# Instruction orders from tables in place of a list scheduler, in a two-layer attention and mixer kernel

## The chip, the cores and the metric

The kernel runs on one core of a Trainium2 chip. The metric is the device time of one execution in microseconds; the time before is the median of three runs. A core has five engines that run their own instruction streams and meet at semaphores: TensorE (PE), VectorE (DVE), ScalarE (ACT), GpSimd (POOL) and SyncE (SP), which here only issues DMAs.

## The reference

Two layers over x of 2048 rows and 448 columns (bfloat16). Each layer is an attention block with 16 heads of 28 columns, then a mixer with an MLP; both read a normed x and add to x.

```
x = x + _A_ref(_layernorm(x), wqkv, wo)
x = x + _B_ref(_layernorm(x), w1, w2, w3, w4)      # the pair of lines twice, with the same weights

_A_ref: q, k, v = split(x @ wqkv);  softmax(q k^T / sqrt(28)) v, heads joined, @ wo
_B_ref: h = gelu(layernorm(x) @ w1)                # 448 -> 448
        hs = (four column groups of h shifted by -1, +1, -2, +2 rows) @ w2
        x1 = x + hs
        return x1 + gelu(layernorm(x1) @ w3) @ w4  # 448 -> 1792 -> 448
```

All of x, the weights and the keys and values stay in the core's memory; x is cut into 16 tiles of 128 rows.

## The kernel before

**The work.** Keys, queries and values are projected tile by tile (`kq_proj`, `v_proj`). Scores are computed transposed: 128 keys by 512 queries (256 in the last units of layer 1) for one head with a 32-row strip of the array (L1243), four heads side by side. ACT takes the exponential of two or three banks of scores at once (L1269, 821 instructions) and writes PT. For 50 tiles DVE computes the exponential instead, with five instructions of its own (`t_dexp`, L1159 to L1172). PT then multiplies the values (L1318, in one of four 32-column strips) into bank 5; `t_norm` divides and transposes, `t_outproj` multiplies with wo and adds to x. The mixer follows in `t_mixA` (w1, tanh form of gelu with L1433 on ACT between DVE's steps), `t_x1` (w2, second norm with a power on POOL, L1568) and `t_mixB` (w3, gelu, w4). The gelus of several tiles are collected into nine long ACT instructions (L1650), since a change between the exponential's and the gelu's function tables costs an ACT_TABLE_LOAD. The last three tiles take their gelus directly from the banks (L1488, L1606).

**Parts of the run.** Before the first exponential lie the loads of x and the weights, squares of the weights for a bound on the scores (`wnorm`, L748, L755), the first norms and transposes, and the first projections. Then the exponentials run one after the other, and all other work of both layers is placed around them. Behind the last exponential the last tiles go through mixer and MLP.

**PSUM.** There are eight banks. The exponentials use two sets in turn, banks 0 to 2 and 3 to 4, by the number of the exponential (`gbank`); bank 5 collects PT times values; everything else takes a bank from 6 and 7, and from others while they are free.

**What sets the order.** The work is written as some hundred generators, each yielding operations with an engine, a planned duration, the buffers read and written, and waits on events. The class `Sched` runs them against a planned clock: at each step it takes the operation that can start first, by rank among equals, and adds it to the list of its engine; `Plan.deps` derives the semaphore waits from the buffers. The engines issue these lists strictly in order. Banks and double buffers (`acq`) are handed out during that run. Two passes give each operation a latest start, which is the next pass's rank; three more passes follow (one for each list in `MOVES`, with random shifts of the ranks at listed times, and the last of them is used), the method `perturb` doing the shifts. In the ready time of some ACT operations there is a margin: 0.3 us for the tanh, 1.0 for the first gelu of a batch. Some operations name an alternative on the second of DVE and ACT, and the scheduler takes it if that engine is free; while the exponentials run, ACT is closed to them. Where PE would stand idle, `keep_pe_busy` puts in matmuls of ones by ones (L1686) into a free bank, up to a share of 0.8 of the last 4 us; their product is not read.

The score matmuls of an exponential (`st_ops`) can be planned from the moment the exponential two before it has released its banks; the rank and a deadline (`dl`) decide what PE does ahead of them.

Of the kernel before, what the change touches and what calls it, by code (L numbers as in the profile page):

```python
# [17 lines left out]
class _Op:  # L18
    __slots__ = ("eng", "fn", "deps", "sig", "cnt", "waits", "dma", "ekey", "vc", "sem", "t_end", "pos", "every", "oid", "dur", "lft", "lst")

    def __init__(self, eng, fn, dma):
# [16 lines left out]
        self.lst = None  # L38


def _split(acc):
    if isinstance(acc, tuple) and len(acc) == 2 and isinstance(acc[0], tuple):
        return acc
    return acc, None

# [122 lines left out]
class Sched:  # L168
# [8 lines left out]
    def __init__(self, P):  # L177
# [4 lines left out]
        self.pe_mode = None  # L182
        self.act_tab = None
# [8 lines left out]
        self.fill = None  # L192
        self.recent = []
        self.clock = 0.0
        self.plan = None
        self.moves = []
# [3 lines left out]
    def spawn(self, gen, prio=5, order=None, parent=None):  # L200
        self.seq += 1
        if parent is None:
            tid = (self.seq,)
        else:
            parent[7] += 1
            tid = parent[6] + (parent[7],)
        self.tasks.append([prio, self.seq if order is None else order + self.seq * 1e-6, gen, None, None, False, tid, 0, 0, None])

    def rank(self, t):
        if self.plan is None:  # L210
            return (t[0], t[1])
        return (self.plan.get((t[6], t[8]), 1e9), t[1])
# [4 lines left out]
    def _advance(self, t, force=False):  # L217
        changed = False
        while True:
# [39 lines left out]
            elif c == "acq":  # L259
# [22 lines left out]
                t[4] = got  # L282
# [8 lines left out]
    def keep_pe_busy(self, until):  # L291
        if self.fill is None:
            return
        dur, fn, banks, key, reads = self.fill
        while self.cur["pe"] + dur + 0.12 < until:
# [21 lines left out]
            self.pe_mode = "plain"  # L317

    def run(self):
        P = self.P  # L320
        while True:
            while self.moves and self.clock >= self.moves[0][0]:
                self.perturb(self.moves.pop(0)[1])
# [23 lines left out]
            for t in self.tasks:  # L347
# [5 lines left out]
                for a in kw0.get("alt", ()):  # L353
                    cands.append(a)
# [8 lines left out]
                for ci, (eng, dur, fn, kw) in enumerate(cands):  # L363
# [13 lines left out]
                    if ci > 0 and (self.cur[eng] > ready + 0.05 or eng in self.reserved):  # L377
                        continue
# [57 lines left out]
            op = P.add(eng, fn, reads, writes, kw.get("deps", ()), dma, t_end)  # L436
            self.live.update(k for k in (_split(a)[0] for a in writes) if k[0] == "ps")
            self.live.difference_update(kw.get("last", ()))
            op.oid = (t[6], t[8])
# [15 lines left out]
    def perturb(self, seed):  # L455
        rng = random.Random(seed)
        if rng.random() < 0.2:
            self.SLACK = rng.choice((0.0, 0.06, 0.12, 0.3))
            self.TOL = rng.choice((0.0, 0.5, 1.5, 4.0))
            self.EPS = rng.choice((0.02, 0.05, 0.12))  # L460
        t = self.clock - self.shift
        lo, hi = t - 30.0, t + rng.choice((10.0, 25.0, 50.0, 90.0))
        depth = rng.choice((0, 1, 2, 3, 9, 9))
        width = rng.choice((1.0, 3.0, 8.0, 20.0))
        frac = rng.choice((0.05, 0.2, 0.5, 1.0))
        plan = self.plan
        sh = {}
        for k, v in plan.items():
            if lo < v < hi and k is not None:
                g = k[0][:depth] if depth else k  # L470
                d = sh.get(g)
                if d is None:
                    d = sh[g] = rng.gauss(0, width) if rng.random() < frac else 0.0
                if d:
                    plan[k] = v + d
# [21 lines left out]
def build_kernel(nc, A_x, A_wqkv, A_wo, B_x, B_w1, B_w2, B_w3, B_w4, out, n_layers=2):  # L497
    S = A_x.shape[1]
    D = 448
# [11 lines left out]
    DEFER = 4  # L511
    OFFL = ((48, 104, 6), (104, 300, 6), (372, 411, 6), (480, 520, 6), (520, 600, 8), (640, 731, 6))
# [6 lines left out]
    MOVES = [  # L519
        [  # L520
# [6 lines left out]
        ],  # L527
        [
# [1248 lines left out]
```

## Time and profile before

| | |
|---|---|
| three runs | 1060.65, 1057.09, 1059.28 us, median 1059.28 |
| span of the profiled execution | 1059.8 us |
| first exponential starts | 27.17 us |
| last large gelu (L1650) ends | 1027.62 us |
| ACT busy | 1015.2 us |
| PE busy | 1020.3 us, of which L1686 143.6 |
| DVE busy | 744.5 us |

The span runs from the first to the last instruction of one execution; it lies 0.5 us above the median and between the runs. The page shows no other time for that execution. A row of a group reads: line, engine, operation, written tile <- read tile, shape, count | busy us, mean ns of one | idle time of that engine just ahead of them, and what ended it. Busy times count overlapping instructions once, so a mean times the count can be above the busy time. A busy PE is not a PE at its peak, since matmuls in different strips run side by side and their ends are modelled. A row of the timeline reads: start, duration, engine, line, operation, and in brackets the idle time before it and what it waited for.

### The profile page before, as it was taken

Reading aid. Unit: us, or ns where it says so; the run is one execution under the profiler, and the core shown is the slowest. Engines: PE = TensorE matmul, PEld = TensorE weight load, DVE = VectorE, ACT = ScalarE, POOL = GpSimd, SP = SyncE. Lnnn points to the kernel's source line nnn. Section 1 sums busy time; section 2 is a strip of 40 time slices with the busy share of each in tenths; the row PEclk is TensorE's granted clock in tenths of the full one; section 3 lists DMA queues with packets and bytes.
Section 4 is the critical chain, followed back from the end, with each engine's and each line's share of the span. In section 5 each row is a group of like instructions: output and inputs, shape, how many; then the busy total and the mean of one; then the engine's idle time right before and its main releaser. Section 6 shows DMA issues by size and latency. Waiting matters only on the chain.

```text
span 1059.8 us, 22773 instructions
## 1 busy us (share of the span) xinstructions
PE 1020.3 (96%) x9869; PEld 397.8 (38%) x9883; DVE 744.5 (70%) x1686; ACT 1015.2 (96%) x933; POOL 57.8 (5%) x80
## 2 busy tenths in 40 slices
PE   9999999999999999999999999989999999999998
PEld 5333332333333333333443443323333333434456
DVE  7966579866987547887689657785879645666454
ACT  5999999999999999999999999999999999999983
POOL 2000000100000001010101000000010000010000
PEclk8999999999999999999999999989999999999999
DMA  4243141001101002110111103211010100110000
GB/s 116 63 122 87 36 122 21 2 16 20 21 2 21 1 1 42 36 21 2 21 41 32 29 8 81 81 41 41 21 36 2 20 15 19 21 22 1 15 6 23
DMA packets 70717, 35.14 MB, mean 33 GB/s; under 512 B 56472, under 2 KB 65048, under 8 KB 70616
## 3 DMA queue, kind: packets, MB, share of 16 engines
q1 hardware_dynamic: 70616, 33.68, 13.4%
q8 instruction: 77, 1.26, 0.5%
q14 instruction: 24, 0.20, 0.1%
HBM read 12.70 MB, written 7.08 MB: 19 GB/s over the span
## 4 chain that ended last, share of the span: by engine, by line
ACT 52%; PE 41%; DVE 4%; DMA 1%; issue 1%; SPq 0%; POOLq 0%; POOL 0%; DVEq 0%
ACT PT L1269 45%; PE ps L1243 11%; PE ps L1318 9%; PE ps L665 9%; PE ps L1686 6%; ACT h2T L1650 4%; PE ps L916 3%; PE ps L668 3%; ACT gt L1433 1%; ACT L1650 1%; ACT L1269 1%; DVE kT L925 1%; DMA xT<-xn 1%; DMA wk_raw<-in_A_wqkv_dram 1%; DVE h2T L1609 0%
## 5 line engine op out<-in xcount | busy, mean ns | idle before, releaser
L1269 ACT ACTIVATE PT<-ps 128x1024 bf16<-128x1024 f32 (+1 forms) x821 | 917.2, 1225 | 10.2 <-PE ps L1243 6.4
L1243 PE MATMUL ps<-qT,kT 32*128 32x512 bf16 x1536 | 240.0, 386 | 13.8 <-ACT PT L1269 11.3
L1318 PE MATMUL ps<-PT,vaug 128*32 128x512 bf16 (+1 forms) x2253 | 250.0, 362 | 2.8 <-ACT PT L1269 1.4
L1686 PE MATMUL ps<-ones_bf 128*128 128x256 bf16 x928 | 143.6, 279 | 2.8 <-DVE hot L698 1.1
L1243 PEld LDWEIGHTS ps<-qT,kT 32*128 32x128 bf16 x1536 | 58.6, 91 | 196.1 <-ACT PT L1269 113.7
L665 PE MATMUL ps<-xT,w 112*128 112x512 bf16 (+5 forms) x623 | 129.2, 325 | 0.5 <-DVE h2T L1609 0.2
L1318 PEld LDWEIGHTS ps<-PT,vaug 128*32 128x32 bf16 x2253 | 65.7, 94 | 118.2 <-issue 66.0
L1609 DVE CAST h2T<-ps 128x512 bf16<-128x512 f32 (+2 forms) x126 | 73.5, 583 | 48.2 <-PE ps L665 40.3
L1686 PEld LDWEIGHTS ps<-ones_bf 128*128 128x128 bf16 x928 | 77.4, 99 | 71.3 <-issue 50.8
L1243 PE MATMUL ps<-kT 32*128 32x256 bf16 (+1 forms) x768 | 80.1, 310 | 2.5 <-ACT PT L1269 1.6
L665 PE MATMUL ps<-w,h2T 128*128 128x448 bf16 x327 | 75.1, 354 | 4.8 <-ACT h2T L1650 3.5
L665 PEld LDWEIGHTS ps<-xT,w 112*128 112x128 bf16 (+1 forms) x623 | 50.2, 103 | 53.6 <-issue 27.7
L1159 DVE TENSOR_SCALAR t<-ps 128x512 int32<-128x512 f32 x50 | 34.2, 684 | 34.4 <-PE ps L1243 34.0
L668 PE MATMUL ps<-xT,w 112*32 112x512 bf16 (+4 forms) x612 | 51.5, 337 | 0.0
L916 PE MATMUL ps<-xT,wq_raw 112*32 112x512 bf16 (+1 forms) x576 | 46.8, 367 | 1.9 <-DVE kT L925 0.9
L1243 PEld LDWEIGHTS ps<-kT 32*128 32x128 bf16 x768 | 21.4, 91 | 64.1 <-ACT PT L1269 32.8
L1650 ACT ACTIVATE h2T<-h2T 128x7168 bf16<-128x7168 bf16 (+2 forms) x9 | 44.8, 5010 | 0.1
L1340 DVE STREAM_TRANSPOSE u_sb<-ps 128x512 f32<-128x512 f32 (+1 forms) x24 | 15.0, 626 | 41.2 <-PE ps L1318 41.2
L916 PE MATMUL ps<-xT,wk_raw 112*32 112x512 bf16 (+3 forms) x640 | 41.8, 346 | 0.8 <-DVE vaug L983 0.3
L665 PEld LDWEIGHTS ps<-w,h2T 128*128 128x128 bf16 x327 | 27.9, 98 | 35.1 <-issue 11.7
L1568 POOL TENSOR_TENSOR mst<-mst,neghalf 128x1 f32<-128x1 f32 x32 | 24.3, 762 | 294.6 <-DVE mst L1566 266.5
L815 DVE BATCH_NORM_STATS2 st<-x_res 128x6 f32<-128x448 bf16 x64 | 38.7, 612 | 1.2 <-DMA x_res<-in_A_x_dram 0.6
(145 smaller groups left out, 1065.2 us busy)
## 6 DMA issues: line engine op xcount, KB each, us to landing
uin<-uscr SPq DMA_DIRECT2D x20, 256.0 KB, 2.6
uscr<-u_sb SPq DMA_DIRECT2D x12, 256.0 KB, 2.0
uscr<-uin SPq DMA_DIRECT2D x8, 256.0 KB, 2.0
out_dram<-uin SPq DMA_DIRECT2D x16, 112.0 KB, 1.7
w<-in_B_w_dram SPq DMA_DIRECT2D x4, 392.0 KB, 4.0
x_res<-in_A_x_dram SPq DMA_DIRECT2D x3, 448.0 KB, 8.9
w<-in_B_w_dram SPq DMA_DIRECT2D x2, 448.0 KB, 7.1
w<-in_B_w_dram SPq DMA_DIRECT2D x4, 196.0 KB, 2.8
```

The lines of the kernel that those rows point to most:

```text
L665: return e.matmul(out=dst(0, m), lhsT=lhs(0, m), rhs=rhs, start=start, stop=stop)
L668: return [e.matmul(out=dst(a, min(m, a + 32)), lhsT=lhs(a, min(m, a + 32)), rhs=rhs, start=start, stop=stop, tile_position=(0, a)) for a i ...
L815: yield op("dve", 0.55, lambda e: e.bn_stats(out=st6[:, t, :], in_=x_res[:, t, :]), reads=[("x", t)], writes=[("st6", t)])
L916: yield op("pe", c_mm(nw) + Sched.COLT, lambda e, b=b, fc=fc, rows=rows: [e.matmul(out=ps[32 * j:32 * j + 32, bi(b), 0:nw], lhsT=w[0:rows, ...
L1159: yield op("dve", 0.06 + c_ps(512), lambda e: e.tensor_scalar(out=t32[:, :], in0=ps[:, bk, :], scalar1=0.0, scalar2=65536.0, op0=ALU.max, ...
L1243: yield op("pe", 0.005 if ph == h else 0.012 + W / 2400.0, lambda e, bk=bk, r0=32 * j, g=g, kc=kc, qt=qt, q0=q0, W=W, c0=W * h: e.matmul(o ...
L1269: yield op("act", e_dur(n), lambda e, b0=b0, p0=p0, cnt=cnt: e.activation(out=PT[:, p0:p0 + cnt, :], in_=ps[:, b0:b0 + cnt, :], func=ACT.E ...
L1318: yield op("pe", nt * 0.054 if item in late else 0.004 + nt * 0.0133, lambda e, j=j, rhs=rhs, vs=vs, i=i: e.matmul(out=ps[32 * j:32 * j + ...
L1568: yield op("pool", 0.57, lambda e, t=t: e.tensor_tensor(out=mst[:, t, R3:R3 + 1], in0=mst[:, t, V3E:V3E + 1], in1=neghalf[:, 0:1], op=ALU. ...
L1609: yield op("dve", c_ps(NW), lambda e, fch=fch, b=b: e.tensor_copy(out=h2T[:, fch, hoff:hoff + NW], in_=ps[:, bi(b), 0:NW]), reads=[("ps", ...
L1650: yield op("act", c_act(14 * NW), lambda e, c0=c0, NW=NW: e.activation(out=h2T[:, :, c0:c0 + NW], in_=h2T[:, :, c0:c0 + NW], func=ACT.Gelu ...
L1686: SC.fill = (0.13, lambda e, b: e.matmul(out=ps[:, bi(b), 0:256], lhsT=ones_bf[:, :], rhs=ones_bf[:, :].unsqueeze(1).to_broadcast([128, 2, ...
```

## The change

The list scheduler still runs, but only to make the operations and the dependency graph: two passes for the latest starts and no random shifts (`MOVES` and `perturb` are gone), no alternatives, no matmuls of ones. Its result is the base. A new method `follow` then makes the program:

- `ENGINE_ORDER` holds for each of PE, ACT, DVE, POOL and SP a text of numbers, which `reorder` reads in pairs: take so many of the base's operations, then skip so many (a negative number steps back). The result is a permutation of the engine's list. The texts hold 10985, 329, 2983, 85 and 157 numbers.
- `OTHER` lists 25 operations, by position in the base's list of 9495, that run on their alternative engine.
- `graph` derives the dependencies from the data, without regard to which bank or buffer the base had given.
- `follow` walks the five orders together; among the engines' next operations it takes the one with the earliest planned start, and hands out bank or buffer then: the one of the free places that has been free longest. In planning PE's time it treats the four strips of the array as separate (`strip_time`), with 0.092 us for a change between whole-array, row-strip and column-strip matmuls (0.09 before). The margins don't enter. The matmuls of ones are put in during this walk; ahead of one that follows strip matmuls the walk leaves the four strips' ends and the 0.092 us.

The rest makes this possible: a name of a place (`Place`) gets its number late, so addresses are computed when the instruction is emitted; the first and last matmul into a strip of bank 5 are known by a count; DVE's exponentials take their PTD buffer by availability and no longer in turn; w3's load and the writes to h2T depend on the read of the squared weights by a key of its own. Which exponentials DVE computes, all tile sizes, batches and the instructions themselves are as before.

```diff
-        for moves in MOVES[:-1]:
-            res = attempt(plan, moves)
-            plan = res[2].latest_starts(res[0])
-        est, P, SC = attempt(plan, MOVES[-1])
+        base = res[2]
+        est, P, SC = base.follow(ENGINE_ORDER, OTHER, MISC)
...
+def reorder(ops, text):
+    out = []
+    i = 0
+    v = [int(x) for x in text.split()]
+    for k in range(0, len(v), 2):
+        out += ops[i:i + v[k]]
+        i += v[k]
+        if k + 1 < len(v):
+            i += v[k + 1]
+    return out
...
+    def follow(self, order, other, banks):
+        for i in other:
+            op = self.P.all[i]
+            reads, writes, kw = op.spec[2:]
+            op.eng, dur, fn, kw2 = op.alts[0]
+            op.spec = (dur, fn, reads, writes, dict(kw, **kw2))
+        ops, after = self.graph()
+        seq = {}
+        for e in ENGS:
+            mine = [op for op in ops if op.eng == e]
+            seq[e] = reorder(mine, order[e]) if e in order else mine
...
+        while len(made) < len(ops):
+            best = None
+            for e in ENGS:
+                if head[e] == len(seq[e]):
+                    continue
+                op = seq[e][head[e]]
...
+                for k in op.toks:
+                    if id(k) not in home:
+                        free = [b for b in places[k.kind] if not (b in started and fixed[b]) and not (b in held and left[held[b]]) and b not in got.values()]
+                        if not free:
+                            break
+                        got[id(k)] = min(free, key=lambda b: freed.get(b, 0.0))
...
+                    if best is None or start < best[0]:
+                        best = (start, e, op, dur, fn, m, extra, reads, writes, got) + ((pe,) if e == "pe" else (None,))
...
+                if e == "pe":
+                    new.keep_pe_busy(start)
...
     def keep_pe_busy(self, until):
-        if self.fill is None:
+        if self.fill is None or not self.filling:
             return
         dur, fn, banks, key, reads = self.fill
+        if self.pe_mode not in (None, "plain"):
+            idle = max(self.strip_free) + self.SW
+            if max(self.cur["pe"], idle) + dur + 0.12 >= until:
+                return
+            self.cur["pe"] = max(self.cur["pe"], idle)
...
+    ENGINE_ORDER = {
+        "act": (
+            "1 2 1 1 1 -4 1 -2 1 4 1 -3 1 2 2 4 1 7 1 -13 1 1 1 -2 1 4 1 -2 1 8 2 -8 1 -2 1 -5 1 5 3 1 1 9 1 -7 3 -4 1 3 3 1 5 1 2 -3 1 2 12 1 5 -6 1 5 17 1 13 -14 "
...
+    OTHER = (
+        44, 61, 62, 63, 66, 110, 127, 131, 133, 136, 154, 165, 169, 171, 177, 189, 222, 238, 248, 274, 346, 415, 9175, 9203, 9385
+    )
```

More of the change, by code (lines that the diff above doesn't have):

```diff
@@ L192, in __init__ @@
         self.fill = None
+        self.filling = True
         self.recent = []
@@ L211, in rank @@
             return (t[0], t[1])
-        return (self.plan.get((t[6], t[8]), 1e9), t[1])
+        spec = t[3]
+        k = spec[5].get("id", t[8]) if spec is not None and len(spec) > 5 else t[8]
+        return (self.plan.get((t[6], k), 1e9), t[1])
     AHEAD = 0.6
@@ new lines, with strip_time @@
+    DL = 0.0035
+    SW = 0.092
+    def strip_time(self, ready, m, dur, kw):
+        sf, tg = list(self.strip_free), list(self.begun)
+        if self.pe_mode is not None and self.pe_mode != m:
+            ready = max([ready] + sf) + self.SW
+            sf = [ready] * 4
+        if m == "plain":
+            end = ready + dur - 0.013
+            return ready, end, end, [end] * 4, tg
+        todo = [(kw["strip"], kw["full"])] if "strip" in kw else [(k, dur - (0.025 if kw.get("mode") == "col4" else 0.026)) for k in range(4)]
+        first, last = None, 0.0
+        for k, w in todo:
+            ready = max(ready, tg[0])
+            t = max(ready + 0.0015, sf[k])
+            tg = sorted(tg + [t])[1:]
+            sf[k] = t + w
+            first = t if first is None else min(first, t)
+            last = max(last, sf[k])
+            ready += self.DL
+        return first, last, ready, sf, tg
@@ L1175, in t_dexp @@
+            for r in (f, x, ti):
                 yield ("rel", r)
             yield ("sig", ("d", n))
+            yield ("wait", ("pvd", n))
+            yield ("rel", to)
         def gbank(n):
@@ L1297, in t_pv, with pv @@
             plan_pv += [(len(kts) - 1, h[1], h[2]) for h in held]
-            lead = {}
-            tail = {}
-            for (_, i, j) in plan_pv:
-                lead.setdefault(j, i)
-                tail[j] = i
+            count = [0, 0, 0, 0]
+            def pv(e, i, j, vs, rhs):
+                count[j] += 1
+                return e.matmul(out=ps[32 * j:32 * j + 32, UBK, 0:128 * nt], lhsT=vaug[:, vs, 32 * (4 * g + j):32 * (4 * g + j) + 32],
+                                rhs=rhs(), start=count[j] == 1, stop=count[j] == len(kts), tile_position=(0, 32 * j))
             free = [c for c in range(2) if L + 1 < n_layers and u == len(UNITS[L]) - 1 and g == 3]
```

440 lines of the change are left out of this document (292 added, 148 removed), and 257 rows, old and new, of tables (ENGINE_ORDER, MOVES).

## The prediction

> **What bounds the kernel now.** I began with the page: busy times, then the costliest groups.
>
> ```profile
> span 1059.8 us, 22773 instructions
> PE 1020.3 (96%) x9869; PEld 397.8 (38%) x9883; DVE 744.5 (70%) x1686; ACT 1015.2 (96%) x933; POOL 57.8 (5%) x80
> L1269 ACT ACTIVATE PT<-ps 128x1024 bf16<-128x1024 f32 (+1 forms) x821 | 917.2, 1225 | 10.2 <-PE ps L1243 6.4
> L1686 PE MATMUL ps<-ones_bf 128*128 128x256 bf16 x928 | 143.6, 279 | 2.8 <-DVE hot L698 1.1
> ```
>
> PE and ACT both show 96%, and they don't mean the same. PE's 1020.3 us contain 928 matmuls of ones by ones that the scheduler puts into gaps (143.6 us); nobody reads them. ACT's 1015.2 us are work: 917.2 of them are the exponentials, whose number the change leaves alone. So ACT is the bound, and an order can only win ACT's idle time, 1059.8 - 1015.2 = 44.6 us. The windows view, cut at the start of the first exponential and at the end of the last large gelu, says where it lies.
>
> ```profile
> 0.00:27.17 27.17, 24.87 (x288) 14.32 (x289) 19.92 (x84) 14.43 (x20) 7.59 (x20) 0.87 0.43 113
> 27.17:1027.63 1000.46, 966.99 (x9315) 363.89 (x9327) 709.37 (x1566) 989.09 (x877) 45.66 (x54) 1.00 0.13 31
> 1027.63:1059.80 32.17, 28.49 (x267) 19.55 (x267) 15.20 (x38) 11.64 (x37) 4.59 (x7) 0.99 0.06 19
> ```
>
> Columns: window, length, then busy time (count) of PE, PEld, DVE, ACT, POOL, granted clock, DMA share, GB/s. ACT idles 27.17 - 14.43 = 12.7 us ahead of the exponentials, 1000.46 - 989.09 = 11.4 in the loop, 32.17 - 11.64 = 20.5 behind it. The loop holds 94% of the time and a quarter of the idle time. Its waits, from the view of waits on ACT between 27 and 1023 us (total, times, longest):
>
> ```profile
> ACT PT L1269 <- PE ps L1243: 6.4, 14, 1.6
> ACT PT L1269 <- PE ps L1318: 1.3, 2, 0.8
> ACT gt L1433 <- DVE gw L1422: 0.7, 3, 0.3
> ACT fct L1085 <- DVE dbc L1083: 0.3, 1, 0.3
> ACT vaug L987 <- PE ps L668: 0.2, 1, 0.2
> ```
>
> They sum to 8.9 us; the other 2.5 us of idle are spread over 877 instructions, which no order touches. Sixteen of 821 exponentials wait, 7.7 us in all, 0.48 on average. Last I read the chain that ended last:
>
> ```profile
> ACT 52%; PE 41%; DVE 4%; DMA 1%; issue 1%; SPq 0%; POOLq 0%; POOL 0%; DVEq 0%
> ACT PT L1269 45%; PE ps L1243 11%; PE ps L1318 9%; PE ps L665 9%; PE ps L1686 6%; ACT h2T L1650 4%; PE ps L916 3%; PE ps L668 3%; ACT gt L1433 1%; ACT L1650 1%; ACT L1269 1%; DVE kT L925 1%; DMA xT<-xn 1%; DMA wk_raw<-in_A_wqkv_dram 1%; DVE h2T L1609 0%
> ```
>
> It gives PE 41%, but 6 of these are the useless L1686: the chain passes over PE where PE and ACT finish together, and doesn't say that PE is short.
>
> **The change, part by part.** The five tables hold 6702 PE, 928 ACT, 1679 DVE, 76 POOL and 110 SP positions. Read as runs of consecutive positions they are 5492, 164, 1491, 42 and 78 runs: PE and DVE are reordered almost instruction by instruction, ACT hardly (one run takes 89 in a row). So ACT does the same work in nearly the same sequence, and what can change is when its inputs are ready.
>
> *The loop.* What a wait is made of, in the timelines of PE and of ACT:
>
> ```profile
> 524.07 1.31 PE L665 MATMUL ps<-w,h2T 128*128 128x448 bf16 x6
> 525.43 1.04 PE L665 MATMUL ps<-xT,w 112*112 112x512 bf16 x4
> 526.40 0.60 PE L1243 MATMUL ps<-qT,kT 32*128 32x512 bf16 x5
> ```
>
> ```profile
> 526.87 1.45 ACT L1269 ACTIVATE PT<-ps 128x1536 bf16<-128x1536 f32 x1 [1.60 <-PE ps L1243]
> ```
>
> PE ran ten matmuls of w4 and w1 (2.3 us) ahead of five score matmuls, and ACT stood for 1.60 us. A position table can put the scores in between, and the ten have room, as the loop's share of L1686 shows (the same windows for that line alone: PE, PEld, clock, DMA share, GB/s):
>
> ```profile
> 27.17:1027.63 1000.46, 135.73 (x876) 71.50 (x876) 1.00 0.13 31
> ```
>
> One part of the 8.9 us is not order:
>
> ```profile
> 700.00:703.00 3.00, 1.84 (x20) 0.49 (x14) 2.90 (x6) 3.00 (x4) 0.00 (x0) 1.00 0.49 121
> 703.00:706.00 3.00, 2.59 (x18) 0.53 (x12) 3.00 (x9) 2.71 (x3) 0.00 (x0) 0.67 0.25 54
> 706.00:709.00 3.00, 3.00 (x18) 0.97 (x16) 1.69 (x5) 2.08 (x3) 0.00 (x0) 0.50 0.00 0
> 709.00:712.00 3.00, 3.00 (x26) 0.83 (x27) 1.74 (x4) 2.45 (x3) 0.00 (x0) 0.69 0.02 5
> ```
>
> Here the granted clock fell to 0.50, after a stretch with PE 61% busy, and ACT lost 0.29 + 0.92 + 0.55 = 1.76 us (its busy column against 3.00). That leaves 8.9 - 1.8 = 7.1 us of placement. Bounds for the gain: 7.1 if all go, nothing if they only move, and below nothing as the second rival says. I take 6.0, near the upper end, since sixteen places are few to mend and PE spends 135.73 us on nothing; one in six survives because a table rests on planned durations.
>
> *The head.* Inputs of the first scores, and what stands between (timelines of DVE, PE, ACT, then the windows view):
>
> ```profile
> 11.68 0.42 DVE L867 COPY xT<-ps 112x512 bf16<-112x512 bf16 x1 [0.38 <-PE ps L862]
> 19.22 0.34 DVE L1195 TENSOR_SCALAR qT<-qT,bcol 128x512 bf16<-128x512 bf16 x1
> ```
>
> ```profile
> 11.60 1.26 PE L755 MATMUL ps<-ones_bf,w 112*112 112x1 bf16 x12
> 12.79 1.90 PE L916 MATMUL ps<-xT,wk_raw 112*32 112x512 bf16 x16
> 26.73 0.60 PE L1243 MATMUL ps<-qT,kT 32*128 32x512 bf16 x5
> ```
>
> ```profile
> 27.17 9.21 ACT L1269 ACTIVATE PT<-ps 128x1536 bf16<-128x1536 f32 x8 [0.16 <-PE ps L1243]
> ```
>
> ```profile
> 19.56:26.73 7.17, 7.07 (x129) 2.81 (x122) 7.16 (x21) 5.25 (x9) 2.87 (x5) 1.00 0.01 2
> ```
>
> The query of the first head group is ready at 19.56, and the scores come at 26.73. But the 7.17 us between are full: PE 7.07, DVE 7.16, ACT 5.25 with evacuations it does in place of DVE. Starting exponentials earlier displaces that work; what is free on ACT is 7.17 - 5.25 = 1.9 us. Another 0.6 lies in the twelve small matmuls of L755 (11.60), which later groups need and which the first projection (12.79) stands behind; its transposed input lands at 11.68 + 0.42 = 12.10. Bounds: 0 (three full engines) and 7.2 (the whole stretch, if every evacuation fits under later work). I take 1.9 + 0.6 = 2.5, near the lower end, as the row of full engines is the nearer one.
>
> *Alternatives.* Before, the scheduler chose between DVE and ACT as it went; now 25 numbered operations take their second engine and all others the first. ACT's table holds 928 operations; before, 933 instructions less 12 table loads make 921. So ACT gets 7 more, DVE 7 fewer (1679 against 1686). Twenty-two of the numbers are at most 415 of 9495, three are beyond 9175, so they lie around the head and tail, where ACT idles. Two kinds that ACT takes already:
>
> ```profile
> L923 ACT ACTIVATE qT<-ps,cols 128x512 bf16<-128x512 f32 x4 | 2.8, 688 | 1.8 <-PE ps L916 1.8
> L987 ACT ACTIVATE vaug<-ps 128x448 bf16<-128x448 f32 x4 | 2.2, 544 | 0.9 <-PE ps L668 0.9
> ```
>
> Bounds: 0 and 7 x 0.69 = 4.8 us. I take 0.7: one of them behind the first exponential, the rest in idle time.
>
> *The tail.* After 1027.63 PE is busy 28.49 of 32.17 us. Its timeline shows the gaps and its end:
>
> ```profile
> 1025.76 1.16 PE L1686 MATMUL ps<-ones_bf 128*128 128x256 bf16 x9
> 1027.68 1.51 PE L668 MATMUL ps<-w,h2T 128*32 128x448 bf16 x28 [0.77 <-ACT h2T L1650]
> 1043.94 0.43 PE L862 MATMUL ps<-ident,xn 128*112 128x128 bf16 x4 [0.77 <-DVE xn L1572]
> 1051.47 5.46 PE L665 MATMUL ps<-w,h2T 128*128 128x448 bf16 x28
> ```
>
> The last matmul ends at 1056.93, so 2.9 us of PE's idle time are the final additions and stores. The gap of 0.77 at 1043.94 can be filled, and the matmuls of ones and the wait just ahead of 1027.68 (1.16 + 0.77 = 1.9) can take work of the last tiles that now stands later. Bounds 0 and 0.8 + 1.9 = 2.7; I take the middle, 1.4.
>
> *Costs at nothing.* Bank and buffer choice changes no instruction's length; what hides a bad choice is that only the exponentials' two bank sets are tight, and those stay fixed by number. SP's and POOL's operations are the same ones in another order. POOL is busy 5%, and SP's loads are hidden by their early issue: in the loop PE's only wait on one is this, and a load moved too far back would cost its whole landing time.
>
> ```profile
> PE ps L916 <- DMA xT<-xn: 0.2, 1, 0.2
> ```
>
> The dependency on the read of the squared weights is long satisfied by the time h2T is written. The filler's new rule asks for more room than the old; matmuls of ones that go missing could bring more clock drops, at 1.8 us each by the window above. I count none, as the rule still fills to 0.8 of four microseconds.
>
> *Sum.* 6.0 + 2.5 + 1.4 - 0.7 = 9.2 us less than 1059.8, so 1050.6 for a profiled execution. Its span is 0.5 above the median of 1059.28, and the median less 9.2 is **1050.1**.
>
> A rule that bears on the tables: the granted clock stood at 0.50 after PE had been busy 1.84 of 3.00 us. The Trainium skill ("TensorE: Matmul & The Clock Gate", the HAM clock gate) says that the gate halves the clock after an idle window of about 3.4 us; the trace agrees with the half, at 0.50. The drop came without an idle window, so the rule is too mild for this kernel; by it alone no drop would come here, and the sum would be 1048.3.
>
> **Rivals.** *Nothing is won* (waits move, head and tail stay full). For it: PE 7.07 and DVE 7.16 of 7.17 in the head, PE 28.49 in the tail. Against: sixteen visible misplacements in the loop. With the tail's 1.4 us alone it gives 1058.
>
> *Slower: a tight order meets other durations.* Every engine now issues strictly by a table, and the planner's margins for ACT's inputs (0.3 us for each tanh, 1.0 for a gelu) have no counterpart there. One late producer then holds ACT, with the next exponential queued behind it, and PE's next scores behind that. For it: the 1.60 us wait shows how little it takes. Against: today's order is just as fixed and waits 16 times in 821. Price: 0.48 us a wait. Head and tail gain 3.2 net; seven further waits eat that, from there on it is slower. At three times today's waits, 32 more: 32 x 0.48 = 15.4, less 3.2, gives 1071. The Trainium skill ("TensorE: Matmul & The Clock Gate", Architectural detail) calls the other engines strict first-in-first-out, which is this mechanism; the 1.60 us wait agrees.
>
> *More is won.* All 7.1 of the loop, 7.2 of the head and 2.7 of the tail: 17.0, so 1042. For it: much of PE's loop is filler. Against: the full head.
>
> *Not what it says:*
>
> ```profile
> L1269 ACT ACT_TABLE_LOAD x5 | 6.4, 1283 | 0.1
> ```
>
> Had the search spread gelus among the exponentials, each extra pair of table loads would cost 2 x 1.28 us; ACT's near-unbroken table speaks against it, so it has no chance of its own.
>
> **How the numbers follow.** Forecast 0.54 (1044 to 1056), more won 0.12, nothing 0.14, slower 0.20. Faster by over 0.3% (below 1056.1; about what a measurement of this kernel can tell from no change) 0.66, same 0.14, slower 0.20. The range reaches from 1040, just under the case of more won, to 1064, into the near part of the slower case (which begins at 1062.5), leaving out about 0.15 above and 0.03 below. PREDICTED's time is the forecast's.
>
> **What would show it.** Loop: the wait of L1269 on L1243 falls from 6.4 to under 2.5 us, on fewer than eight occasions. Head: first exponential at or before 25 us, with less than 1 us of new ACT idle before 60. Tail: from the last large gelu to the end under 31 us. ACT busy within 5 us of 1015. The prediction is wrong if ACT's idle time in the loop is above 11.4 us, if clock windows below 1.0 appear more than twice after 30 us, or if ACT's busy time itself falls or rises by more than 5 us.

## The result and the profile after

The changed kernel takes 1064.90 us (median of 15 runs, 1060.08 to 1068.88), the kernel before beside it 1060.65 (15 runs, 1056.62 to 1063.01): ratio 1.0044, 95% interval 1.0027 to 1.006. The forecast was 1050.1 and "faster"; it is slower by 4.2 us, and above the range.

The page of the changed kernel, its engines, its exponentials, its matmuls of ones and the granted clock in 40 slices of 26.6 us:

```profile
span 1062.9 us, 23784 instructions
PE 990.1 (93%) x10412; PEld 372.2 (35%) x10412; DVE 737.8 (69%) x1679; ACT 1012.7 (95%) x940; POOL 54.4 (5%) x80
PEclk8998959999999999999999999999999999999999
L1740 ACT ACTIVATE PT<-ps 128x1024 bf16<-128x1024 f32 (+1 forms) x821 | 912.7, 1256 | 15.6 <-PE ps L1773 7.9
L2161 PE MATMUL ps<-ones_bf 128*128 128x256 bf16 x470 | 83.7, 284 | 4.3 <-DVE hot L1153 2.5
```

ACT's busy time fell by 2.5 us (1015.2 before), so 5.6 us more of the span are idle ACT (50.2 against 44.6). The page shows two signs of where: the exponentials' idle time is now mostly put down to L1773 (PT times values; it was the scores), and the clock has a slice at half, the sixth, about 133 to 159 us. The windows view, cut as for the kernel before:

```profile
0.00:29.89 29.89, 22.17 (x268) 12.39 (x272) 17.65 (x76) 15.15 (x21) 7.52 (x20) 0.89 0.57 152
29.89:1031.77 1001.88, 939.67 (x9881) 340.43 (x9874) 705.79 (x1571) 986.03 (x880) 42.80 (x54) 0.98 0.13 30
1031.77:1062.90 31.13, 28.24 (x267) 19.39 (x267) 14.37 (x34) 11.48 (x40) 4.08 (x7) 1.00 0.06 19
```

The head is 2.7 us longer, the tail 1.0 shorter, and the loop idles ACT for 1001.88 - 986.03 = 15.9 us, against 11.4. One sum over the loop hides two opposite things. Cut again at 112 and 200 us, and ended at 1013, first the kernel before, then the changed one:

```profile
27.17:112.00 84.83, 81.20 (x802) 27.59 (x807) 66.45 (x168) 83.57 (x77) 2.10 (x2) 1.00 0.36 93
112.00:200.00 88.00, 85.72 (x735) 30.96 (x737) 64.81 (x122) 87.11 (x83) 2.13 (x2) 1.00 0.19 47
200.00:1013.00 813.00, 786.75 (x7601) 298.25 (x7601) 570.53 (x1259) 803.81 (x708) 41.25 (x49) 1.00 0.11 24
```

```profile
29.89:112.00 82.11, 71.69 (x748) 23.55 (x741) 56.69 (x152) 74.80 (x69) 2.01 (x2) 0.96 0.41 99
112.00:200.00 88.00, 78.70 (x605) 21.86 (x603) 58.40 (x113) 81.59 (x77) 2.45 (x2) 0.84 0.11 27
200.00:1013.00 813.00, 771.55 (x8210) 285.16 (x8204) 579.44 (x1278) 810.89 (x722) 38.29 (x49) 1.00 0.11 24
```

ACT's idle time (length less its busy column) goes 1.26 to 7.31 in the first stretch, 0.89 to 6.41 in the second, and 9.19 to 2.11 in the long third one. There the forecast came true, at 7.1 us; the first 200 us took it back, and more.

**The first stretch** is one stall. Following it back through the timelines of ACT, PE, DVE and SP's queue (start, length, what; in brackets the idle time before it and what ended it):

```profile
102.91 1.45 ACT L1740 ACTIVATE PT<-ps 128x1536 bf16<-128x1536 f32 x1 [6.41 <-PE ps L1773]
```

```profile
102.25 0.61 PE L1773 MATMUL ps<-PT,vaug 128*32 128x512 bf16 x3 [6.22 <-DVE uin L1818]
```

```profile
101.44 0.75 DVE L1818 SCALAR_TENSOR_TENSOR uin<-uin,fct,ps 128x512 f32<-128x512 f32 x1 [6.96 <-DMA uin<-uscr]
```

```profile
89.44 0.42 SPq L1261 DMA_DIRECT2D wo_pad<-in_A_wo_dram  x1
89.91 2.45 SPq L1261 DMA_DIRECT2D w<-in_B_w_dram  x5
92.40 0.42 SPq L1261 DMA_DIRECT2D wo_pad<-in_A_wo_dram  x1
92.94 0.50 SPq L1674 DMA_DIRECT2D uin<-uscr  x1
```

The last line is the load that all wait for: a partial sum of attention, which comes back from memory to be added to what bank 5 holds. It is issued at 92.94, and DVE, which waits for it, starts at 101.44, 8.5 us later. Ahead of it SP issues seven weight loads in a row. The page's list of DMA issues gives the median of all 20 loads of this kind (KB each, us from issue to landing):

```profile
uin<-uscr SPq DMA_DIRECT2D x20, 256.0 KB, 2.7
```

The kernel before issues its weight loads one at a time, each behind such a load; its SP queue at the same place:

```profile
87.11 0.32 SPq L1204 DMA_DIRECT2D uin<-uscr  x1
87.48 0.43 SPq L806 DMA_DIRECT2D w<-in_B_w_dram  x1
90.84 0.32 SPq L1356 DMA_DIRECT2D uscr<-uin  x1
92.85 0.32 SPq L1204 DMA_DIRECT2D uin<-uscr  x1
```

While ACT stands, the DMA engines are full (the windows view in steps of 3 us; the last two columns are the DMA share and GB/s):

```profile
94.00:97.00 3.00, 1.54 (x11) 0.69 (x11) 0.48 (x2) 2.50 (x3) 0.00 (x0) 1.00 1.13 274
97.00:100.00 3.00, 0.00 (x0) 0.00 (x0) 0.00 (x0) 0.00 (x0) 0.00 (x0) 0.75 1.01 236
```

The Trainium skill ("DMA: Bandwidth & Descriptors", Queues, rings and completion order) says that SP's DMAs share one row of rings, whose descriptors are consumed in order; the trace is in line with it, 8.5 us for the load with seven ahead of it. The planner, which made the tables' base and walks them, gives each weight load 7.0 us and this load 3.0, each by itself (`dma_time` at L1261 and L1674), so to it such a pile costs nothing.

**The second stretch** idles at half clock, without a stall (steps of 3 us):

```profile
133.00:136.00 3.00, 2.34 (x21) 0.60 (x18) 2.77 (x5) 3.00 (x4) 0.00 (x0) 1.00 0.00 0
136.00:139.00 3.00, 2.47 (x22) 0.67 (x23) 2.96 (x6) 2.73 (x3) 0.00 (x0) 0.51 0.00 0
139.00:142.00 3.00, 3.00 (x22) 0.68 (x20) 2.76 (x6) 2.37 (x2) 0.00 (x0) 0.50 0.36 93
```

The clock falls after a window in which PE was busy for 2.34 of 3.00 us, and stays at about half to 163 us. At that clock PE doesn't keep up with ACT: from 139 to 142 us it is busy all the time, and ACT idles for 0.63 us.

### The profile page after: what moved, and what is told of

The parts are those of the page before. It is cut to its first block, busy times and chain, and to the rows that moved or that the text cites. A ratio compares the mean times of both kernels' runs of the same rounds, so it can differ in the third digit from the quotient of the medians.

```text
span 1062.9 us, 23784 instructions
## 1 busy us (share of the span) xinstructions
PE 990.1 (93%) x10412; PEld 372.2 (35%) x10412; DVE 737.8 (69%) x1679; ACT 1012.7 (95%) x940; POOL 54.4 (5%) x80
## 4 chain that ended last, share of the span: by engine, by line
ACT 81%; PE 13%; DMA 2%; DVE 2%; SPq 1%; issue 0%; DVEq 0%
ACT PT L1740 75%; ACT h2T L2126 4%; PE ps L1120 4%; PE ps L1714 3%; PE ps L1123 2%; PE ps L1773 2%; PE ps L1383 2%; ACT gt L1910 1%; DMA wv<-in_A_wqkv_dram 1%; DMA uin<-uscr 1%; SPq L1261 1%; ACT L2126 1%; ACT L1740 0%; PE ps L2161 0%; SPq L1246 0%
## 5 line engine op out<-in xcount | busy, mean ns | idle before, releaser
L1740 ACT ACTIVATE PT<-ps 128x1024 bf16<-128x1024 f32 (+1 forms) x821 | 912.7, 1256 | 15.6 <-PE ps L1773 7.9
L1773 PE MATMUL ps<-PT,vaug 128*32 128x512 bf16 (+1 forms) x2253 | 296.0, 366 | 9.0 <-DVE uin L1818 6.2
L1773 PEld LDWEIGHTS ps<-PT,vaug 128*32 128x32 bf16 x2253 | 84.3, 95 | 135.4 <-issue 85.2
L1123 PE MATMUL ps<-xT,w 112*32 112x512 bf16 (+3 forms) x1224 | 95.4, 344 | 0.2 <-DVE h2T L2086 0.2
L1120 PE MATMUL ps<-xT,w 112*128 112x512 bf16 (+6 forms) x470 | 94.1, 317 | 0.6 <-DVE h2T L2086 0.5
L2161 PE MATMUL ps<-ones_bf 128*128 128x256 bf16 x470 | 83.7, 284 | 4.3 <-DVE hot L1153 2.5
L1123 PE MATMUL ps<-w,h2T 128*32 128x448 bf16 x924 | 57.1, 353 | 2.2 <-ACT h2T L2126 2.1
L2161 PEld LDWEIGHTS ps<-ones_bf 128*128 128x128 bf16 x470 | 38.5, 99 | 47.8 <-issue 27.3
L1120 PE MATMUL ps<-w,h2T 128*128 128x448 bf16 x217 | 52.2, 354 | 0.0
L1120 PEld LDWEIGHTS ps<-xT,w 112*128 112x128 bf16 (+1 forms) x470 | 38.2, 104 | 38.9 <-issue 20.5
L1123 PEld LDWEIGHTS ps<-xT,w 112*32 112x32 bf16 (+1 forms) x1224 | 37.6, 95 | 15.6 <-DVE h2T L2086 2.0
```

The source lines that it names most:

```text
L1120: return e.matmul(out=dst(0, m), lhsT=lhs(0, m), rhs=rhs() if callable(rhs) else rhs, start=start, stop=stop)
L1123: return [e.matmul(out=dst(a, min(m, a + 32)), lhsT=lhs(a, min(m, a + 32)), rhs=rhs() if callable(rhs) else rhs, start=start, stop=stop, t ...
L1740: yield op("act", e_dur(n), lambda e, b0=b0, p0=p0, cnt=cnt: e.activation(out=PT[:, p0:p0 + cnt, :], in_=ps[:, b0:b0 + cnt, :], func=ACT.E ...
L1773: return e.matmul(out=ps[32 * j:32 * j + 32, UBK, 0:128 * nt], lhsT=vaug[:, vs, 32 * (4 * g + j):32 * (4 * g + j) + 32], rhs=rhs(), start= ...
L2161: SC.fill = (0.13, lambda e, b: e.matmul(out=ps[:, bi(b), 0:256], lhsT=ones_bf[:, :], rhs=ones_bf[:, :].unsqueeze(1).to_broadcast([128, 2, ...
```

## The experiments

The theory (A): two groups of moved weight loads cost the time, the seven ahead of the load of the partial sum, and at the start five that stand among the loads of x and ahead of wv. Rival B: too few matmuls of ones (470 against 928) let the clock fall. Rival C: the tight order of PE itself makes ACT wait.

All idle times below are ACT's, in the stretches used above, worked out as there from the windows view of each profile (the first from the first exponential on). e9, e10 and e12 are second executions of a kernel, to show how much one profile says.

| kernel | us, median (runs) | ratio to before, 95% | first exponential | idle to 112 | 112 to 200 | 200 to 1013 |
|---|---|---|---|---|---|---|
| before | 1060.65 (15) | | 27.17 | 1.26 | 0.89 | 9.19 |
| e12, before again | 1060.25 (1) | | 25.76 | 1.38 | 0.89 | 9.07 |
| after | 1064.90 (15) | 1.0044 (1.0027 to 1.006) | 29.89 | 7.31 | 6.41 | 2.11 |
| e9, after again | 1062.79 (1) | | 25.58 | 9.79 | 2.02 | 6.04 |
| e8, head moved | 1057.87 (12) | 0.999 (0.9968 to 1.0013) | 22.43 | 7.45 | 3.86 | 2.06 |
| e1, middle moved | 1053.69 (10) | 0.9947 (0.9925 to 0.9969) | 28.52 | 0.12 | 3.83 | 2.04 |
| e10, e1 again | 1056.61 (1) | | 25.50 | 0.12 | 9.92 | 2.07 |
| e2, both moved | 1047.14 (4) | 0.986 (0.9843 to 0.9877) | 24.14 | 0.13 | 2.75 | 2.07 |
| e3, old filler rule | 1079.99 (4) | 1.0176 (1.016 to 1.0191) | 27.59 | 7.44 | 6.88 | 10.48 |
| e4, e2 and old rule | 1071.11 (4) | 1.0086 (1.0054 to 1.0118) | 22.21 | 0.88 | 9.21 | 10.05 |
| e6, e2 and 719 fillers | 1052.27 (4) | 0.9912 (0.9884 to 0.9941) | 23.20 | 0.12 | 4.23 | 6.11 |
| e7, before and a bunch | 1065.57 (10) | 1.0061 (1.0037 to 1.0084) | 24.61 | 6.30 | 0.78 | 7.35 |
| e11, before, 710 fillers | 1056.61 (12) | 0.9969 (0.9956 to 0.9982) | 25.49 | 1.25 | 0.00 | 8.12 |

### The loads moved (e1, e2, e8)

In `follow`, ahead of the walk, SP's list is put together anew from runs of itself, all else as changed. e1:

```diff
             seq[e] = reorder(mine, order[e]) if e in order else mine
+            if e == "sp":
+                seq[e] = [op for a, b in ((0, 28), (35, 36), (28, 30), (36, 38), (30, 32), (38, 39), (42, 43), (32, 35), (43, 44), (39, 42), (44, 110)) for op in seq[e][a:b]]
```

e8 does the head alone: runs (0, 4), (6, 7), (8, 10), (12, 13), (4, 6), (7, 8), (10, 12), (13, 110). e2 does both.

> Only SP's order is changed: ten of the weight loads that stand bunched around 90 and 111 us go behind later loads of uin, at most three in a row; everything else as in the changed kernel (median 1064.9, profiled span 1062.9, ACT waits 7.9 us on L1773 in four places, 6.4 in one). Theory A, the bunch delays the load of uin behind it: the 6.4 us wait on ACT at 96 us goes, and with it the half clock that follows the idle PE there; about 7 us less, 1056 to 1059. Theory B, the loss is the clock alone, from too few matmuls of ones: the wait at 96 may go, but the stretch at half clock from 136 to 163 us stays, some 6 us of ACT idle. Theory C, the tight PE order itself waits whatever SP does: the time stays within 2 us of 1064.9.

> As the run before, and in the head SP issues the inputs first: wk, x, wq, the rest of x, wv, and then the five weight loads that now stand ahead of wv. Theory A: the first exponential moves from 29.9 us to 27 or earlier, since wv and x land sooner (PE waited on wv, ACT 5.3 us on the keys), so 2 to 3 us less than the run with the middle alone. Rival: the head is bound by its chain of engines, not by the loads; then the first exponential stays at about 29 and the time is the same as with the middle alone.

> The changed kernel with only the head of SP's list altered: the x loads and wv first, then the five weight loads; the seven weight loads ahead of the uin load near 91 us stay where the change put them. If the two loads' delays add (head 6.5 us by the step from the middle alone to both, middle about 11), this gives about 1058.5, with the first exponential at 24 us and the 6 us stall of PV on uin still there, some 5 us earlier. If the head is worth only what its start shows (first exponential 29.89 to 24.14 in the profiles, less the evacuations that then stand later), 3 to 6 us, it gives 1059 to 1062. If the long half-clock stretch at 136 to 163 us follows from the stall, it is there again, some 5 us earlier; if it belongs to the late start, it is gone and the time comes to about 1052.

e1 is 11.2 us below the changed kernel, more than was expected, and its stall is gone: in the table 0.12 us instead of 7.31. The stall itself is thus 7.2 us; the rest lies, in this pair of profiles, in the second stretch (2.6) and in the first exponential's start (1.4), which both change from one execution to the next, as the second profiles below show. Its waits on ACT over the whole loop (us, times, longest) were

```profile
ACT PT L1742 <- PE ps L1716: 3.9, 8, 0.8
ACT PT L1742 <- PE ps L1775: 1.3, 3, 0.6
```

e2 is another 6.5 below it, and 13.7 below the kernel before beside it (1060.80): the fastest of all here. SP's queue in its first microseconds, where the changed kernel had wv last, at 10.27:

```profile
2.80 1.69 SPq L1248 DMA_DIRECT2D x_res<-in_A_x_dram  x3
4.53 1.14 SPq L1244 DMA_DIRECT2D wv<-in_A_wqkv_dram  x1
5.72 5.20 SPq L1263 DMA_DIRECT2D w<-in_B_w_dram  x5
```

e8, the head alone, is 7.0 below the changed kernel. 11.2 and 7.0 make 18.2, and both together gave 17.8: within a few us, which is what the intervals allow, the two add, as the theory has it (by the ratios, each against the kernel before beside it, 10.3 and 5.7 against 19.5). Without the edit the first exponential stands at 29.89, 25.58, 28.52, 25.50 and 27.59 us (mean 27.4), with it at 24.14, 22.43, 22.21 and 23.20 (mean 23.0), which is 4.4 of the 7.0 us. (e5, below, starts at 26.71, without matmuls of ones.) Part of these 4.4 may be the clock: from 10 to 22 us it was granted at 0.78 to 0.86 in the five without the edit, and at 1.00 in three of the four with it. At the same 0.86, e2 starts at 24.14 and four without it between 25.50 and 28.52, at 26.8 on average, which is 2.7 us.

### The bunch put into the kernel before (e7)

The next five weight loads (`wl`) are issued right ahead of the load of a partial sum at 92.85 us (`at`); `sp` is SP's list.

```diff
...
+        some = [op for op in wl if sp.index(op) > sp.index(at)][0:5]
+        for ops in (sp, P.all):
+            rest = [op for op in ops if op not in some]
+            k = rest.index(at)
+            ops[:] = rest[:k] + some + rest[k:]
...
```

> The kernel before with one edit to its SP order: the next five weight loads are issued right ahead of the load of uin at 92.85 us, as in the changed kernel. Theory A: that load lands 6 to 9 us later, DVE, PE and ACT stand for 4 to 7 us, perhaps with a spell of half clock behind it; 1065 to 1072, ratio 1.004 to 1.010. Rival, the stall needs the tight orders of the changed kernel: the kernel before has room and stays within 2 us of 1060.8.

It is 3.7 us slower than the kernel before beside it (1061.89), with every other order as it was. Its profile is of its fastest run, 1062.18. SP's queue, the longest wait of PE there, and that of ACT behind it:

```profile
89.39 2.33 SPq L806 DMA_DIRECT2D w<-in_B_w_dram  x5
91.77 0.50 SPq L1204 DMA_DIRECT2D uin<-uscr  x1
93.03 6.77 SPq L856 DMA_TRANSPOSE xT<-xn  x1
```

```profile
PE ps L916 <- DMA xT<-xn: 3.9, 1, 3.9
```

```profile
103.53 1.02 ACT L1269 ACTIVATE PT<-ps 128x1024 bf16<-128x1024 f32 x1 [3.86 <-PE ps L1243]
```

The idle time up to 112 us rises from 1.3 to 6.3, as in the changed kernel. Which load is late differs: here PE waits for the transposed input issued behind the bunch. So a bunch of weight loads is enough to stop the engines; the new order of PE isn't needed for it.

### Second profiles (e9, e10, e12)

The changed kernel, e1 and the kernel before once more, without an edit.

> The changed kernel itself, for a second profile. If the half-clock stretch of 27 us behind the 6 us stall belongs to the order, it stands again at 136 to 163 us with about 6.6 us of idle ScalarE; if it is chance of that execution, the windows between 130 and 170 us differ and the span differs with them by up to 7 us.

> The kernel with the middle loads moved, for a second profile. Its first profile had granted clocks of 0.83, 0.83 and 0.91 in the three windows of 20 us from 120 us. If shorter drops there belong to the order, they stand again and ScalarE idles about 4 us in 30 to 180 us; if the clock there is chance, they differ.

> The kernel before itself, for a second profile beside the last. Idle ScalarE was 1.26 us up to 112 us, 0.89 to 200 and 9.19 to 1013 in its first profile; if these belong to its order, they stand again within 2 us, and the first exponential's start (27.17) moves by up to 3 us as it did in the other kernels.

The stall stands again, a little longer, on ACT's timeline of e9:

```profile
99.38 1.45 ACT L1740 ACTIVATE PT<-ps 128x1536 bf16<-128x1536 f32 x1 [7.20 <-PE ps L1773]
```

The long stretch at half clock does not. The changed kernel's first profile, then e9, from 140 to 160 us:

```profile
140.00:160.00 20.00, 18.43 (x95) 3.71 (x87) 9.92 (x17) 15.75 (x15) 0.00 (x0) 0.50 0.08 26
```

```profile
140.00:160.00 20.00, 16.07 (x125) 4.50 (x125) 12.52 (x23) 19.57 (x19) 0.00 (x0) 0.93 0.06 14
```

e9 has a drop elsewhere, which the first profile hasn't (a step of 50 us), and e10 one from 180 to 200 us, where e1's first profile has a clock of 1.00:

```profile
450.00:500.00 50.00, 47.36 (x410) 15.49 (x403) 36.94 (x84) 46.02 (x43) 2.56 (x4) 0.87 0.06 12
```

```profile
180.00:200.00 20.00, 19.84 (x106) 5.44 (x104) 14.41 (x29) 15.78 (x16) 1.44 (x1) 0.67 0.01 1
```

The kernel before repeats to 0.12 us in each stretch. So the new order makes drops between 112 and 200 us likely (every profile of it idles there for 2 to 10 us, those of the kernel before for 0.89), but where they fall and how long they last changes from one execution to the next. The first profile's 27 us at half clock are one such draw, and need not be explained by the stall ahead of it: e10 has none of the stall and idles 9.92 us.

### The matmuls of ones (e3, e4, e5, e6, e11)

e3 takes the added clause out of `keep_pe_busy`, which gives 718 matmuls of ones; e4 does so in e2:

```diff
-        if self.pe_mode not in (None, "plain"):
-            idle = max(self.strip_free) + self.SW
-            if max(self.cur["pe"], idle) + dur + 0.12 >= until:
-                return
-            self.cur["pe"] = max(self.cur["pe"], idle)
```

e5 leaves all of them out of e2 (`new.fill = None`); e6 keeps the new clause in e2, with margins of 0.0 in place of 0.12 and `TARGET = 0.95` in place of 0.8 (the share up to which gaps are filled), which gives 719.

> Only the filler's rule is that of before: the clause that waits for the end of the strip matmuls is taken out, so 718 matmuls of ones are put in for 470 (928 before); all tables as in the changed kernel. Theory B, a thin PE drops the clock: the half clock from 136 to 163 us goes and with it about 6 us of ACT idle, 1057 to 1060; the DMA wait at 96 us stays at 6 us. Theory A: that stretch comes from the shock at 97 us and its aftermath, the clock stays low there, no gain. Rival: fillers planned over strips that are still busy delay the scores; ACT's waits on L1714 rise above 15 us and the time is above 1066.

> SP's order mended in the middle and the head, and the filler's old rule. If A and B both hold and add up: 6.4 + 6 + 2.5 us less than 1064.9, about 1050, the time forecast for the order tables. If the filler costs what it gains: as with SP mended alone.

> As the run with SP's order mended in both places (1047.1, ratio 0.986), with no matmuls of ones at all (470 there), which leaves only unread work out. If they hold the clock: more windows at half clock in the loop than the two drops between 123 and 147 us there, at some 2 us of ACT idle each; 1055 or more. If they do nothing: 1047 within 2 us, or less, since PE is then freer.

> As the run with SP's order mended in both places, with 719 matmuls of ones for 470, all still placed by the new rule behind the end of the strip matmuls (the 0.12 us of margin at their end is taken out and the share raised to 0.95). The run with the old rule had 718 and was 24 us slower. If the number of fillers is what costs: about 1070 again. If it is their place, over strips that are still busy and close ahead of the scores: 1043 to 1052, and the two clock drops between 123 and 147 us may go.

B falls as far as it speaks of the number in the whole kernel: with 718 of them instead of 470 the changed kernel takes 15 us more (e3), and e2 takes 24 us more (e4, which was expected at 1050, or at e2's time), and the idle time from 112 to 200 us doesn't go (6.88, 9.21 and, in e6, 4.23). What counts is where they stand. e4 and e6 have the same number within one, and lie 18.8 us apart. Their exponentials, e4 first, and e2's for comparison:

```profile
L1737 ACT ACTIVATE PT<-ps 128x1024 bf16<-128x1024 f32 (+1 forms) x821 | 920.4, 1237 | 19.9 <-PE ps L1711 12.6 <-PE ps L1770 3.4
```

```profile
L1742 ACT ACTIVATE PT<-ps 128x1024 bf16<-128x1024 f32 (+1 forms) x821 | 911.9, 1256 | 4.7 <-PE ps L1716 3.3 <-PE ps L1775 0.8
```

We read this as matmuls of ones that stand behind strip matmuls and delay the next scores a little, at many places: of the 24 us between e2 and e4, 8.0 are idle time from 200 us on (10.05 against 2.07), 6.5 idle time from 112 to 200, and 8.5 stand in the exponentials' busy time. With none at all (e5) the kernel takes 1102.16 us (ratio 1.0379, interval 1.0318 to 1.044), the mean granted clock of its profiled run, the slowest of four, is 0.897, and the clock falls all over the span:

```profile
PEclk9997678869988899997999999997899899558999
```

So they do hold the clock, as B says; 470 in the right places do so from 200 us on, in five of the six profiles with that number (e9 is the sixth).

That raises a doubt: was it the clause, and not the tables, that emptied the loop's waits? e11 comes near the clause in the kernel before: all engines' work in the same order, but of its 928 matmuls of ones the first of each run that follows strip matmuls is out, 218 in all.

```diff
...
-            self.P.add("pe", lambda e, b=pick: fn(e, b), reads, [key(pick)], t_end=t + dur)
+            op = self.P.add("pe", lambda e, b=pick: fn(e, b), reads, [key(pick)], t_end=t + dur)
+            if self.pe_mode not in (None, "plain"):
+                self.dropped.append(op)
...
+        P.ops["pe"] = [op for op in P.ops["pe"] if op not in drop]
...
```

> The kernel before with the same order of all its work on every engine, but 218 of its 928 matmuls of ones taken out: the first of each run that follows strip matmuls. The changed kernel's rule keeps matmuls of ones from strips that are still busy, and with the old rule put back its loop idles ScalarE as long as the kernel before does (10.05 us against 9.19 between 200 and 1013 us; 2.07 with the new rule). If that rule alone is what emptied the loop's waits, the kernel before now idles ScalarE under 5 us in that stretch and takes 4 to 8 us less, 1053 to 1057. If the order of scores and other matmuls did it, the stretch keeps 7 to 11 us of idle time and the time is within 2 us of the kernel before. If the missing matmuls bring clock drops, it is 2 to 6 us slower.

It is 3.1 us faster than the kernel before (ratio 0.9969), but its idle time from 200 us on stays at 8.12. Its waits there, then those of the kernel before, of e2 and of e4 in the same stretch:

```profile
ACT PT L1272 <- PE ps L1246: 4.2, 7, 1.6
ACT PT L1272 <- PE ps L1321: 1.3, 2, 0.8
```

```profile
ACT PT L1269 <- PE ps L1243: 4.6, 8, 1.6
ACT PT L1269 <- PE ps L1318: 1.3, 2, 0.8
```

```profile
ACT PT L1742 <- PE ps L1716: 1.2, 3, 0.5
ACT PT L1742 <- PE ps L1775: 0.2, 1, 0.2
```

```profile
ACT PT L1737 <- PE ps L1711: 6.1, 21, 0.9
ACT PT L1737 <- PE ps L1770: 0.8, 4, 0.2
```

So matmuls of ones taken out aren't enough: e11 keeps the long waits, up to 1.6 us each. The tables aren't enough either: e4 has them with the old rule, and in place of the long waits it has 21 short ones, as much idle time (10.05) as the kernel before. Only tables and clause together bring 2.07. Taking those matmuls out does give the other part, ACT's busy time: 1012.7 us in e11 against 1015.2, as in the changed kernel.

## Why the prediction was wrong

With two profiles of each (e9, e12) the sum of the change is: first exponential 1.3 us later, idle time +7.2 to 112 us, +3.3 to 200, -5.1 to 1013, ACT's busy time in the loop -2.9 (986.2 against 989.2 on average), tail -1.0. That makes 2.8, about the difference of the mean spans (2.9); the medians of 15 runs differ by 4.2.

**The step that failed** is the one under "Costs at nothing": "SP's loads are hidden by their early issue". It named the right price itself, "a load moved too far back would cost its whole landing time", had the count that should have warned (SP's 110 positions read as 78 runs), and then priced the loads by PE's wait in the old order, where one weight load stands between two such loads. In the new order seven do, and the engine that waits for the load is DVE (6.96 us). The runs put that at 11.2 us (e1) and, in the head, 7.0 (e8); 17.8 together (e2). With these two groups put back behind the urgent loads the kernel takes 1047.14, 3.0 under the forecast of 1050.1. That it comes so near is in part luck: it holds 4.0 us of ACT's busy time in the loop (985.14 against 989.09), which the forecast didn't have.

**The loop (6.0 forecast).** Right in mechanism with the new rule for the matmuls of ones, without which it isn't there (e4), and somewhat small. In e2 ACT idles 0.13 + 2.75 + 2.07 = 5.0 us up to 1013 us, the kernel before 1.26 + 0.89 + 9.19 = 11.3, which is 6.4 less, clock drops included. The exponentials' waits on scores are 1.2 us from 200 us on, 4.6 in the kernel before. The idle time outside the listed waits, which the prediction held to be out of an order's reach, shrank there too, from 2.3 us (9.19 less waits of 6.9) to 0.7 (2.07 less 1.4). In the changed kernel this gain is there too from 200 us on (7.1 in the first profile, 3.2 in e9, where one more drop near 450 to 500 us stands), and the stall hid it.

**The head (2.5).** Failed with the same step: the five weight loads delayed the first exponential's inputs. The profiles with the head of before (before, e7, e11, e12) start it at 27.17, 24.61, 25.49 and 25.76, on average 25.8; with the changed head it is 27.4, which is 1.6 later; with the loads put right 23.0, which is 2.8 earlier, about what the forecast gave the head. At equal clock from 10 to 22 us it is less: 1.5 at 0.86 (e2 against e11 and e12) and 2.0 at 1.00 (e4, e6 and e8 against e7). One pair of profiles can't size this: the first pair said 2.7 later, e9 against the first of before 1.6 earlier.

**The tail (1.4).** 31.13 us against 32.17: 1.0.

**The alternatives (+0.7 on ACT).** ACT's busy time was to rise by less than a microsecond and fell by 2.5. The seven operations are there (940 instructions against 933), but the 821 exponentials cover 4.5 us less although the mean of one rose from 1225 to 1256 ns. The durations add to 821 x 1.256 = 1031 us and cover 912.7: 144 ns of each lie beside its neighbour, against 108 before (1006 and 917.2). We read this as exponentials that start under their predecessor's end when their scores are ready earlier; e4, with the same order of ACT and later scores, has 116 ns. No run isolates it. The Trainium skill ("ScalarE: Activation LUTs", What ACT_TABLE_LOAD costs) says that ACTIVATEs back to back overlap by some 93 ns; the trace shows more, and it is part of what an order can win. "An order can only win ACT's idle time" was therefore too narrow.

**The clock drops (none counted).** Put at nothing because "the rule still fills to 0.8 of four microseconds"; the count fell from 928 to 470, and 0.9 us of idle time between 112 and 200 us became 2 to 10. The criterion "clock windows below 1.0 more than twice after 30 us" was met. They weren't caused by the number of matmuls of ones in the whole kernel alone: e6 has 719 and idles there for 4.23.

**The rivals.** The slower rival (1071) had the right shape, one late producer, with everything behind it in strict order, but the wrong producer: it spoke of planned durations of tanh and gelu, and of many waits of 0.48 us. It was one wait of 6.4 us on a DMA. Rival C above, its kin, falls for the changed kernel as it is: from 200 us on its tight order waits less than the old.

**What stays open.** Why the new order lets the clock fall between 112 and 200 us wasn't isolated; PE is busy for 78.1 of 88 us there in e2, for 85.7 in the kernel before, but e11, with 82.78, shows no idle ACT at all. One rival wasn't tested: too few matmuls of ones in that stretch. The windows view of that line alone, from 112 to 200 us, counts 150 in the kernel before and 113 in e11, where the clock is 1.00, but 47 to 63 in the profiles with 470 in all and 84 to 93 in e3, e4 and e6, where it is 0.81 to 0.94. More of them put there, with the tables as they are, would decide it. And 2.6 of the head's 7.0 us aren't seen in the first exponential's start; the spread of the second stretch is large enough to cover them.

## What to carry to other kernels

When a change reorders instructions by the thousand, look at the DMA queue's order first: it has few entries (110 here), and seven of them ahead of one load stopped ACT for more than 6 us. Ask of every load that something waits for how many bytes stand ahead of it in its queue; a planner that times each DMA by itself doesn't see that. And take a second profile of the same kernel before a difference of 2 to 5 us at one place of one trace is explained.

## What the runs showed of the hardware

- A load of 256 KB that takes 2.7 us at the median took 8.5 behind seven weight loads on the same queue.
- The clock fell without an idle window of PE: after PE had been busy for 2.34 of 3.00 us, it stood at about half for 27 us in one execution and not in another of the same kernel. No threshold follows: two earlier windows with 2.39 and 2.42 of 3.00 us (from 112 and 121 us) kept a clock of 1.00.
- Practically the same number of matmuls of ones (718 and 719), put in at other places, made 18.8 us of difference.
- The first exponential of one and the same kernel started at 29.89 us in one execution and at 25.58 in another; from 10 to 22 us the granted clock was 0.78 in the first and 0.86 in the second.
